# A decode block on one core: w3 in one DMA behind wo's row 12, the moved wq columns in two DMAs, x for the residual in two parts on the sync queue

## The chip, the core and the metric

The kernel runs on one core of a Trainium2 chip. The metric is device microseconds of one execution, median of several runs. The profile is one such execution; its span (136.1 us before) leaves out a little of what the time holds.

## The reference

Four tokens pass through one pre-norm block: layer norm, attention over the last 2048 positions of a cache, a residual, layer norm, a gated MLP, a residual. Everything is bf16 at the interface.

```
x: (4, 1, 1024)   wq: (1024, 4096)   k, v cache: (4, 4, 8192, 128), last 2048 used
wo: (4096, 1024)  w1, w3: (1024, 3584)  w2: (3584, 1024)

h  = x + softmax(q k^T * 128**-0.5) v @ wo      with q = layernorm(x) @ wq, 32 heads on 4 kv heads
h2 = h + (silu(layernorm(h) @ w1) * (layernorm(h) @ w3)) @ w2
```

With four tokens every weight is used once, so 55.6 MB have to be read for very little arithmetic.

## The kernel before

All weights and the cache pass through one ring of 160 KiB in each partition. A list says what is loaded where, in order; a call of `load_next` puts the next loads on the sync queue. The framework adds the waits: a load into bytes that are still to be read waits for their last reader. The last 512 columns of the last wq row of each partition are loaded apart from the rest, in 128 pieces of 1 KB on few DMA engines; these are the "moved columns" (`side` in the code).

```python
CE = 512
SETS = [(0, 5, 4), (80, 3, 2), (104, 3, 2)]

def load_side(r0, ne, ns):      # the last 512 columns of each partition's last wq row, as rows of their own
    t = ktpool.tile([P, JG * QD * 16], BF16, tag="kT")
    rows = A_wq[r0 * KC : (r0 + ne * 4 * ns) * KC, N_Q - CE : N_Q]
    rows = rows.rearrange("(t i k) n -> k i t n", i=ne, k=KC)[KC - 1]
    nc.sync.dma_start(out=t[: ne * 4, : ns * CE], in_=rows)
    ...
plan = [
    ("wq", load_rows, (0, wq_v, N_Q, 0, 4)),
    ("side", load_side, SETS[0]), ("side", load_side, SETS[1]), ("side", load_side, SETS[2]),
    ("wq", load_tail, (32 * KIB, wq_v, N_Q, 4, 4)),          # without those 512 columns
    ("k", ...), ("k", ...), ("v", ...),                      # two loads each
    ("v", load_kv, (0, A_v_cache, 2)),
    ("wo", load_rows, (32 * KIB, wo_v, D, 0, 32)),
    ("w1", load_rows, (96 * KIB, w1_v, N_F, 0, 8)),
    ("w3", load_rows, (0, w3_v, N_F, 0, 4)),
    ("w3", load_rows, (28 * KIB, w3_v, N_F, 4, 4)),
    ("w2", load_rows, (56 * KIB, w2_v, D, 0, 17)),
    ... # three more parts of w2
]
x_sb = act.tile([B, D], BF16)
nc.scalar.dma_start(out=x_sb[:], in_=x_flat)                 # x for the layer norm
load_next(8)
...
x_q = act.tile([P, CG], BF16)                                # x for the residual
nc.vector.memset(x_q[:], 0.0)
nc.scalar.dma_start(out=x_q[0:P:RS, :], in_=x_flat.rearrange("b (j c) -> j b c", j=JG))
...
# attention output, over b and j:   OT_ps += v[b][:, j, :] x P
        if b % BS == BS - 1:
            load_next()                                      # w1, then w3's first half
...
# y_ps += o4[i] x wo[i], i = 0..31
        if i == 11:
            load_next()                                      # w3's second half
load_next()                                                  # w2, first 17 rows
...
gate_up("w1", g_ps)                                          # after row 3: load_next(3), the rest of w2
...                                                          # silu on ACT and DVE
gate_up("w3", u_ps)
nc.vector.tensor_tensor(out=hg[:], in0=u_ps[:, :, :HF], in1=gs[:], op=ALU.mult)
nc.vector.transpose(out=hgT..., in_=hg...)                   # then y2 += hgT[i] x w2[i], i = 0..27
```

## Time and profile before

| | before |
|---|---|
| time, median of 3 (range) | 137.84 us (137.83 to 138.2) |
| bytes read from HBM | 55.59 MB, mean 409 GB/s over the span |
| complete landing of: first wq rows / wq tail | 12.84 / 23.57 us |
| wo / w1 | 82.02 / 98.91 us |
| w3, first and second half | 107.36 / 115.82 us |
| first part of w2 / last part of w2 | 126.08 / 132.79 us |

The landings are read from the semaphore increments in the trace: each DMA engine that carries part of a transfer adds one when its part is in, so a transfer over all engines shows 16 times, of which the last one counts. The page's lines and the stretches that carry the argument stand in the prediction below, with what to see in each. Two more lines of the kernel before will be needed, the start of the statistics and the first q matmuls in the timeline (columns: start, length, engine, line, operation, in brackets the idle time ahead and what ended it):

```profile
2.81 0.68 DVE L177 BATCH_NORM_STATS2 stats<-x_sb 4x6 f32<-4x512 bf16 x1 [0.33 <-DMA x_sb<-in_A_x_dram]
...
12.88 0.60 PE L260 MATMUL q_ps<-ring,xnT 128*4 128x512 bf16 x4 [6.49 <-DMA ring<-in_A_wq_dram]
```

The PE had idled for 6.49 us when wq came, so x was there long before.

### The profile page before, as it was taken

How to read it: one execution, taken by the hardware profiler on the slowest of the kernel's cores; microseconds unless marked ns; L12 is line 12 of the kernel's file. 1: busy time of each engine (PE TensorE's matmuls, PEld its weight loads, DVE VectorE, ACT ScalarE, POOL GpSimd, SP SyncE). 2: the span in 40 equal slices, each digit the busy share in tenths (PEclk: the TensorE clock that was granted, in tenths of full speed). 3: DMA queues.
4: the chain of work that ended last, by engine and by line, in shares of the span. 5: the costliest groups of instructions: out<-in, count | busy, mean ns of one | idle time of the engine just before them, and what ended most of it. 6: DMA issues, size and time to landing. Idle time of an engine off the chain costs nothing.

```text
span 136.1 us, 2438 instructions
## 1 busy us (share of the span) xinstructions
PE 72.9 (54%) x1096; PEld 45.1 (33%) x1096; DVE 44.1 (32%) x81; ACT 31.0 (23%) x36; POOL 1.7 (1%) x8
## 2 busy tenths in 40 slices
PE   0202980979898989800545906791096440900881
PEld 0200220267474737400034905470042220300760
DVE  5830000044252434471983001206100695080010
ACT  3000000016555555518376200000003300000000
POOL 5000000000000000000000000000000000000000
PEclk9999999999999999996555555589658686555589
DMA  5999999999999999999979999989899999989970
GB/s 157 463 464 413 414 401 419 443 419 438 419 434 434 424 443 419 429 527 458 482 328 443 482 409 405 477 388 460 354 421 426 455 438 451 430 389 403 434 292 5
DMA packets 2789, 55.75 MB, mean 410 GB/s; under 512 B 311, under 2 KB 471, under 8 KB 731
## 3 DMA queue, kind: packets, MB, share of 16 engines
q1 hardware_dynamic: 2731, 55.58, 95.5%
q8 instruction: 8, 0.13, 0.3%
q10 hardware_dynamic: 48, 0.02, 0.1%
q14 instruction: 2, 0.02, 0.0%
HBM read 55.59 MB, written 0.01 MB: 409 GB/s over the span
## 4 chain that ended last, share of the span: by engine, by line
DMA 55%; PE 23%; ACT 11%; DVE 5%; SPq 2%; issue 1%; ACTq 0%
DMA ring<-in_B_w_dram 40%; DMA ring<-in_A_wq_dram 15%; PE kt_ps L316 10%; ACT kT L322 5%; PE scores_ps L301 5%; ACT z L357 3%; PE q_ps L260 3%; SPq L120 2%; PE g_ps L456 2%; DVE rmax L333 2%; ACT Pm L338 2%; PE OT_ps L379 2%; DVE pT L347 1%; DVE z L353 1%; ACT L338 1%
## 5 line engine op out<-in xcount | busy, mean ns | idle before, releaser
L322 ACT COPY kT<-kt_ps 128x1024 bf16<-128x1024 bf16 x16 | 15.9, 1013 | 13.0 <-PE kt_ps L316 13.0
L316 PE MATMUL kt_ps<-ident,ring 128*128 128x128 bf16 x256 | 17.6, 228 | 0.0
L316 PEld LDWEIGHTS <-ring 128*128 128x128 bf16 x256 | 15.7, 103 | 4.9 <-issue 4.9
L320 DVE COPY kT<-kt_ps 128x1024 bf16<-128x1024 bf16 x16 | 11.1, 692 | 16.0 <-PE kt_ps L316 16.0
L260 PE MATMUL q_ps<-ring,xnT 128*4 128x512 bf16 x63 | 7.2, 627 | 10.1 <-DMA ring<-in_A_wq_dram 10.1
L379 PE MATMUL OT_ps<-z,ring 128*128 128x32 bf16 x256 | 7.5, 188 | 9.3 <-ACT z L357 5.0
L456 PEld LDWEIGHTS <-hnT 128*32 128x32 bf16 x128 | 5.3, 137 | 19.4 <-issue 16.7
L301 PE MATMUL scores_ps<-kT,qz 128*32 128x512 bf16 x64 | 9.9, 609 | 2.9 <-ACT kT L322 2.9
L456 PE MATMUL u_ps<-ring,hnT 128*32 128x448 bf16 x64 | 6.2, 567 | 8.6 <-DMA ring<-in_B_w_dram 8.6
L379 PEld LDWEIGHTS <-ring 128*128 128x128 bf16 x256 | 7.4, 105 | 10.0 <-issue 9.9
L456 PE MATMUL g_ps<-ring,hnT 128*32 128x448 bf16 x64 | 5.3, 515 | 5.4 <-DMA ring<-in_B_w_dram 5.4
L489 PEld LDWEIGHTS <-hgT 128*32 128x32 bf16 x156 | 4.5, 120 | 9.6 <-issue 8.8
L489 PE MATMUL y_ps<-ring,hgT 128*32 128x256 bf16 x68 | 3.8, 418 | 7.2 <-DMA ring<-in_B_w_dram 7.2
L278 DVE TENSOR_SCALAR q_sb<-q_ps 128x512 bf16<-128x512 f32 x1 | 0.7, 692 | 19.2 <-PE q_ps L260 19.2
L260 PEld LDWEIGHTS <-xnT 128*4 128x4 bf16 x63 | 2.0, 116 | 14.4 <-issue 14.3
L511 ACT CAST res<-yb_ps 128x128 bf16<-128x128 f32 x1 | 0.3, 266 | 26.6 <-PE yb_ps L489 26.6
L357 ACT ACTIVATE z<-pt_ps,mask 128x512 bf16<-128x512 f32 x8 | 5.3, 687 | 3.5 <-DVE z L353 3.5
L349 PE MATMUL pt_ps<-pT,perm 128*128 128x512 bf16 x4 | 2.4, 608 | 6.8 <-DVE pT L347 6.8
L279 ACT ACTIVATE q_sb<-q_ps 128x512 bf16<-128x512 f32 x1 | 0.6, 597 | 23.3 <-DVE q_sb L278 23.3
L353 DVE TENSOR_SCALAR z<-pt_ps,mask 128x512 bf16<-128x512 f32 x8 | 5.5, 741 | 1.2 <-ACT z L357 0.8
L470 DVE RECIPROCAL eg<-eg 128x896 f32<-128x896 f32 x1 | 5.8, 5753 | 0.0
L408 PE MATMUL y_ps<-ring,o 128*32 128x256 bf16 x128 | 5.3, 345 | 0.8 <-DVE o L395 0.8
(85 smaller groups left out, 54.7 us busy)
## 6 DMA issues: line engine op xcount, KB each, us to landing
ring<-in_A_k_cache_dram SPq DMA_DIRECT2D x4, 2048.0 KB, 25.3
ring<-in_A_v_cache_dram SPq DMA_DIRECT2D x4, 2048.0 KB, 39.1
ring<-in_B_w_dram SPq DMA_DIRECT2D x1, 7168.0 KB
ring<-in_B_w_dram SPq DMA_DIRECT2D x2, 3584.0 KB, 23.3
ring<-in_B_w_dram SPq DMA_DIRECT2D x1, 4352.0 KB
ring<-in_A_wq_dram SPq DMA_DIRECT2D x1, 4096.0 KB, 12.1
ring<-in_A_wq_dram SPq DMA_DIRECT2D x1, 3968.0 KB, 19.8
ring<-in_B_w_dram SPq DMA_DIRECT2D x1, 1792.0 KB
```

What stands on the lines that cost most here:

```text
L260: nc.tensor.matmul(q_ps[QD * g : QD * g + B, hf * 512 : hf * 512 + n], lhsT=xnT[:, kc, :], rhs=wq_t[:, c0 : c0 + n], start=(kc == 0), stop ...
L301: nc.tensor.matmul(scores_ps[QD * g : QD * (g + 1), n * 512 : (n + 1) * 512], lhsT=qz_v[:, z0 : z0 + QD], rhs=kT_v[:, g, :, :], start=(b = ...
L316: nc.tensor.transpose(out=kt_ps[:, jj, :], in_=k_v[:, n * NJ + t * TB + jj, :], identity=ident[:])
L320: nc.vector.tensor_copy(out=kT[:, t * TB : (t + 1) * TB, :], in_=kt_ps[:])
L322: nc.scalar.copy(out=kT[:, t * TB : (t + 1) * TB, :], in_=kt_ps[:])
L353: nc.vector.tensor_scalar(out=z[:, :, g, :], in0=pt_ps[:], scalar1=mask[:, g : g + 1], scalar2=None, op0=ALU.mult)
L357: nc.scalar.mul(out=z[:, :, g, :], in_=pt_ps[:], mul=mask[:, g : g + 1])
L379: nc.tensor.matmul(OT_ps[:, b, :], lhsT=loaded["v"][b][:, j, :], rhs=PTz[j // NJ][:, (j % NJ) * B + b, :, :], start=(j == 0), stop=(j == J ...
L408: nc.tensor.matmul(y_ps[QD * j : QD * (j + 1), :], lhsT=o4[:, i, :, :].rearrange("p b s -> p (b s)"), rhs=loaded["wo"][i][:, j * CG : (j + ...
L456: nc.tensor.matmul(out_ps[QD * j : QD * (j + 1), hf, :HF], lhsT=hnT[:, k, :], rhs=loaded[kind][k][:, c0 : c0 + HF], start=(k == 0), stop=( ...
L470: nc.vector.reciprocal(out=eg[:], in_=eg[:])
L489: nc.tensor.matmul(out_ps[QD * j : QD * (j + 1), :n], lhsT=hgT[:, i, :], rhs=loaded["w2"][i][:, j * CG + c0 : j * CG + c0 + n], **kw,)
```

## The change

It has three parts that share one idea: fewer and differently placed DMA issues for the same bytes. w3 becomes one transfer, which may only start when wo's first 12 rows, whose place it takes, are used up. Two of the three moved-column loads are joined. x for the layer norm comes in two halves on the scalar queue, and x for the residual moves to the sync queue, in two parts.

```diff
-    SETS = [(0, 5, 4), (80, 3, 2), (104, 3, 2)]
+    SETS = [(0, 5, 4), (80, 3, 4)]
...
-        ("side", load_side, SETS[2]),
...
-        ("w3", load_rows, (0, w3_v, N_F, 0, 4)),
-        ("w3", load_rows, (28 * KIB, w3_v, N_F, 4, 4)),
+        ("w3", load_rows, (0, w3_v, N_F, 0, 8)),
...
-    nc.scalar.dma_start(out=x_sb[:], in_=x_flat)
-    load_next(8)
+    for c in range(2):
+        nc.scalar.dma_start(out=x_sb[:, c * 512 : (c + 1) * 512], in_=x_flat[:, c * 512 : (c + 1) * 512])
+    load_next(7)
...
-    nc.scalar.dma_start(out=x_q[0:P:RS, :], in_=x_flat.rearrange("b (j c) -> j b c", j=JG))
+    for c in range(2):
+        nc.sync.dma_start(
+            out=x_q[c * 2 * QD : (c + 1) * 2 * QD : RS, :],
+            in_=x_flat.rearrange("b (j c) -> j b c", j=JG)[2 * c : 2 * c + 2],
+        )
...
-        if b % BS == BS - 1:
+        if b == 1:
             load_next()
```

## The prediction

> **What bounds the kernel now.** I read the page's slices first, to see which resource is full over the whole span; then stretches between landings, to see whether it is full everywhere; then the sync queue's issues and waits, to see how early each transfer is queued; last the timeline around the places that the change touches.
>
> ```profile
> PE 72.9 (54%) x1096; PEld 45.1 (33%) x1096; DVE 44.1 (32%) x81; ACT 31.0 (23%) x36; POOL 1.7 (1%) x8
> ...
> DMA  5999999999999999999979999989899999989970
> ```
>
> No engine is busy for much over half of the span, while the DMA row is at 9 from the second slice to the last but two. The stretches (columns: from:to, length, busy time of PE, PEld, DVE, ACT, POOL with counts, granted clock, DMA share, GB/s) say at what rate:
>
> ```profile
> 23.60:62.70 39.10, 30.72 (x359) 19.51 (x358) 14.50 (x20) 18.49 (x19) 0.00 (x0) 1.00 1.02 436
> 62.70:82.00 19.30, 8.28 (x192) 6.17 (x192) 8.27 (x14) 8.15 (x12) 0.00 (x0) 0.50 1.01 438
> ...
> 98.90:115.90 17.00, 8.38 (x100) 4.02 (x103) 7.47 (x3) 2.20 (x2) 0.00 (x0) 0.70 1.01 435
> 115.90:131.00 15.10, 7.59 (x140) 4.89 (x143) 3.22 (x3) 0.00 (x0) 0.00 (x0) 0.51 0.97 417
> 131.00:132.80 1.80, 1.58 (x60) 1.23 (x49) 0.00 (x0) 0.00 (x0) 0.00 (x0) 1.00 0.48 187
> ```
>
> The stream runs at about 435 GB/s and the last stretch falls to 187. The landing events in the trace (one semaphore increment for each DMA engine that took part) sharpen this: wo is complete at 82.02 us and w1 at 98.91, so w1's 7.34 MB took 16.89 us, or 435 GB/s; w3's halves land at 107.36 and 115.82 (8.46 us for 3.67 MB, 434 GB/s). So every transfer starts where the last one ends, and **the end is the sum of the bytes over a saturated stream**. It is the slowest DMA engine that counts: the first wq load's 16 increments lie 0.47 us apart, all later loads' about 1.8 us, to the last one (131.00 to 132.79). What lies between is the moved wq columns: 128 pieces of 1 KB, 46 ns each in the trace, on few engines. Their landings show 5 increments for the first set and 3 for each of the others, so the engines in all three carry 16 + 8 + 8 = 32 pieces, 32 x 46 ns = 1.5 us more than the others. That lag stays to the end and explains the 187 GB/s.
>
> The chain of waits seems to say otherwise for the middle (K transposes, softmax), but it follows w1 back to its issue at 75.79 us, and w1 could not have moved before wo was in at 82.02: the compute chain has some 6 us to spare. The sync queue's issues and waits:
>
> ```profile
> 75.79 0.33 SPq L94 DMA_DIRECT2D ring<-in_B_w_dram  x1
> ...
> SPq L94 <- PE OT_ps L379: 7.8, 1, 7.8
> ...
> 89.03 0.33 SPq L94 DMA_DIRECT2D ring<-in_B_w_dram  x1
> ...
> SPq L94 <- PE y_ps L408: 4.6, 1, 4.6
> ...
> 91.27 0.33 SPq L94 DMA_DIRECT2D ring<-in_B_w_dram  x1
> ```
>
> w1 goes out at 75.79, w3's second half at 89.03 (it waited for wo's row 12), the first part of w2 at 91.27; the queue does not need w3 until w1 is in at 98.91.
>
> **What the Trainium skill says.** All on the page "DMA: Bandwidth & Descriptors". Its Specifications give a fabric ceiling of 435 GB/s and an HBM limit near 358 for a core; the trace sits on the first (435 for w1), the second is not seen here. "Queues, rings and completion order" says that a DMA engine takes turns between queues packet by packet. The trace agrees: the residual's x, issued on the scalar queue at 1.35 us, has all 20 of its packets only between 6 and 11.3 us, one turn per wq packet (about 1.2 us each):
>
> ```profile
> q10 hardware_dynamic: 20, 0.01, 0.6%
> ```
>
> "Why a DMA increments its semaphore by 16 and not by 1" says that the number of engines is the largest count up to 16 that divides the slowest dimension of both sides; the 5 and 3 increments above fit sets with 5 and 3 row groups. "Issuing engines are not separate DMA queues" says that another queue saves only issue time; so moving x cannot add bandwidth, and no run yet shows it here.
>
> **The change part by part.**
>
> 1. *w3 in one DMA behind wo's row 12.* Bytes equal. It is issued where the second half was, about 89.0 us, and must be queued before 98.91: 9.9 us spare, no gap. It lands where the second half did, about 115.8. What it costs is early work:
>
> ```profile
> 107.40 3.01 PE L456 MATMUL u_ps<-ring,hnT 128*32 128x448 bf16 x32 [3.13 <-DMA ring<-in_B_w_dram]
> ...
> 115.86 3.18 PE L456 MATMUL u_ps<-ring,hnT 128*32 128x448 bf16 x32 [5.44 <-DMA ring<-in_B_w_dram]
> ...
> 119.08 1.09 DVE L475 TENSOR_TENSOR hg<-u_ps,gs 128x896 bf16<-128x896 f32 x1 [4.86 <-PE u_ps L456]
> 120.21 1.70 DVE L478 STREAM_TRANSPOSE hgT<-hg 128x896 bf16<-128x896 bf16 x1
> 126.18 3.55 PEld L489 LDWEIGHTS <-hgT 128*32 128x32 bf16 x69 [7.95 <-issue]
> 126.21 3.82 PE L489 MATMUL y_ps<-ring,hgT 128*32 128x256 bf16 x68 [7.17 <-DMA ring<-in_B_w_dram]
> ```
>
> The first 32 matmuls now wait with the others: 115.86 + 3.01 + 3.18 = 122.05, product 1.09 and transpose 1.70 with two gaps of 0.04, so hgT is ready near 124.9 instead of 121.91. The down projection waits for w2's first part until 126.08 anyway: **3.0 us later, 1.2 us still spare**, cost 0.
>
> 2. *The moved columns in two DMAs.* The second set has 3 row groups still, so by the rule it stays on 3 engines with 16 pieces each: 16 + 16 = 32 as before. One issue of 0.72 us on the sync queue goes, beside the first wq transfer: gain 0. Two small DVE copies go (one of xs, one of xsT), ahead of use: gain 0.
>
> 3. *x for the statistics in two halves on the scalar queue.* The first is issued at 0.73 as before; the second at about 1.35, where the residual's x was, and should meet the same turns: data near 6.1, increment near 7.4, landed near 7.7 instead of 2.8 us. From there the second statistics, the normalisation and the transposes to xnT took 6.31 - 2.81 = 3.5 us, less 0.66 for the first half: xnT near 10.6. The first wq load lands at 12.84: **some 4.3 us later, about 2.2 us still spare**, cost 0.
>
> 4. *The residual's x on the sync queue.* The compiled order has both parts after the second v load, and each DMA reuses the completion semaphore of the one eight before it. So the second part waits for the wq tail (23.57), and the last two v loads for the first two k loads (28.43 and 33.42), up to 13 us later than now. They are not needed in the stream before the second v load is in at 52.73: 19 us spare, cost 0. Each part has 8 rows from 2 groups, so 2 engines with 4 pieces of 512 B each; both parts make 8 pieces on engines that are already among the late ones, against 4 on the scalar queue before: 4 x 27 ns = +0.11 us. Increments cost 9 ns each: two more for these, two fewer for the dropped side and w3 loads, 0.
>
> Sum: 0 + 0 + 0 + 0.1 = **+0.1 us, 137.9 us**.
>
> **The rivals.** (a) *The down projection becomes bound by the PE.* hgT would have to slip by more than 1.2 us beyond the estimate. For it: the granted clock is 0.50 there, and 1.2 us is little. Against: both matmul times used are measured, the second one at 0.50, so nothing slower is in sight. It would add perhaps 0.5 us, since the last parts of w2 leave the PE slack as well. (b) *x arrives too late.* It would take over two more turns of 1.2 us; even then the q matmuls have slack before the wq tail at 23.57, so 0. (c) *The queue runs dry* because w3 waits for wo's row or v waits for k: 9.9 and 19 us speak against; a gap would cost its full length. (d) *A gain*, from fewer transfers or a scalar queue that gets out of the way of the wq load: at 435 GB/s with equal bytes I see at most tenths, -0.3 us or so.
>
> **Range and chances.** The three runs of before span 137.83 to 138.2, so 0.4 us is noise; with (a) upwards and (d) downwards, 137.5 to 138.5. Two per cent is 2.8 us, which no step comes near: within 2% has 0.97, slower 0.02 for an unseen gap in the stream, faster 0.01.
>
> **What would show it.** One u_ps group of 64 matmuls from about 115.8 us, hgT ready near 125 and y_ps still released by the DMA near 126.2; the second x_sb statistics near 7.7 us and q_ps still released by wq near 12.9; 432 to 438 GB/s between landings; v issues at about 28 and 33 us. The prediction is wrong if y_ps is released by hgT, if the DMA row shows a new gap, or if the lag of the last landing (1.8 us) has changed by over 0.3 us.

## The result, and the profile after

The changed kernel takes 137.94 us (median of 6 runs, 137.79 to 137.97), the kernel before 137.88 us in 6 runs. The ratio is 0.9999 with a 95% interval of 0.9986 to 1.0012. Ratios here are the mean time of one kernel's fast runs over that of the other's fast runs of the same rounds, so they are not quite the ratio of the medians. The change costs and gains nothing that can be measured: less than 0.2 us either way.

The page's engine line and DMA row of the changed kernel:

```profile
PE 72.3 (53%) x1096; PEld 46.1 (34%) x1096; DVE 43.9 (32%) x79; ACT 31.0 (23%) x36; POOL 1.7 (1%) x8
...
DMA  5999999999999999999989999989989899999970
```

The DMA row is as full as before. The stretches say the same (columns as in the prediction):

```profile
23.60:62.70 39.10, 31.16 (x359) 19.89 (x358) 14.49 (x20) 18.01 (x19) 0.00 (x0) 0.85 1.02 436
62.70:82.00 19.30, 8.28 (x192) 6.16 (x192) 8.27 (x14) 8.63 (x12) 0.00 (x0) 0.50 1.02 441
...
131.00:132.80 1.80, 1.80 (x70) 1.57 (x64) 0.00 (x0) 0.00 (x0) 0.00 (x0) 0.85 0.46 179
```

435 GB/s or a little over in the middle, and the thin last stretch, 179 GB/s, is there again. What has moved is work inside the slack. The second half of the gate (the product with w3, and its transpose to hgT, which the down projection y_ps needs) in the timeline:

```profile
115.70 5.95 PE L459 MATMUL u_ps<-ring,hnT 128*32 128x448 bf16 x64 [11.03 <-DMA ring<-in_B_w_dram]
121.71 1.09 DVE L478 TENSOR_TENSOR hg<-u_ps,gs 128x896 bf16<-128x896 f32 x1 [7.09 <-PE u_ps L459]
122.83 1.70 DVE L481 STREAM_TRANSPOSE hgT<-hg 128x896 bf16<-128x896 bf16 x1
126.06 3.82 PE L492 MATMUL y_ps<-ring,hgT 128*32 128x256 bf16 x68 [4.40 <-DMA ring<-in_B_w_dram]
```

All 64 matmuls now wait for w3 and run in one group, hgT is ready at 122.83 + 1.70 = 124.53 us (121.91 before), and y_ps is still released by the DMA, at 126.06 us. The head of the timeline, and what the scalar queue carried in the stretch from 6 to 11.3 us (packets, MB, share):

```profile
7.92 0.68 DVE L180 BATCH_NORM_STATS2 stats<-x_sb 4x6 f32<-4x512 bf16 x1 [4.90 <-DMA x_sb<-in_A_x_dram]
...
12.94 0.60 PE L263 MATMUL q_ps<-ring,xnT 128*4 128x512 bf16 x4 [2.03 <-DMA ring<-in_A_wq_dram]
```

```profile
q10 hardware_dynamic: 8, 0.00, 0.3%
```

Eight packets, 4 of data and 4 increments, are x's second half: it is used at 7.92 us instead of about 3.5 us, and the PE's idle time ahead of q shrinks from 6.49 to 2.03 us, but wq still ends it. The sync queue's issues:

```profile
33.41 0.56 SPq L102 DMA_DIRECT2D ring<-in_A_v_cache_dram  x1
...
76.27 0.33 SPq L94 DMA_DIRECT2D ring<-in_B_w_dram  x1
...
88.76 0.33 SPq L94 DMA_DIRECT2D ring<-in_B_w_dram  x1
```

The last v load goes out at 33.41 us (23.63 before), w1 at 76.27, w3 at 88.76, all ahead of need. The residual's x shows two increments for each of its parts (two engines each), the last ones at 52.67 and 52.86 us; it is used after 91 us.

### The profile page after: what moved, and what is told of

Its sections match the earlier page's. It is cut to its first block, busy times and chain, and to the rows that moved or that the text cites. A ratio compares the mean times of both kernels' runs of the same rounds, so it can differ in the third digit from the quotient of the medians.

```text
span 136.0 us, 2436 instructions
## 1 busy us (share of the span) xinstructions
PE 72.3 (53%) x1096; PEld 46.1 (34%) x1096; DVE 43.9 (32%) x79; ACT 31.0 (23%) x36; POOL 1.7 (1%) x8
## 4 chain that ended last, share of the span: by engine, by line
DMA 54%; PE 25%; ACT 11%; DVE 5%; SPq 2%; issue 1%; ACTq 0%
DMA ring<-in_B_w_dram 38%; DMA ring<-in_A_wq_dram 15%; PE kt_ps L319 11%; ACT kT L325 5%; PE scores_ps L304 5%; ACT z L360 3%; PE q_ps L263 3%; DVE rmax L336 2%; ACT Pm L341 2%; PE OT_ps L382 2%; DVE pT L350 1%; SPq L120 1%; PE g_ps L459 1%; DVE z L356 1%; ACT L341 1%
## 5 line engine op out<-in xcount | busy, mean ns | idle before, releaser
L263 PE MATMUL q_ps<-ring,xnT 128*4 128x512 bf16 x63 | 6.7, 595 | 7.8 <-DMA ring<-in_A_wq_dram 7.8
L459 PE MATMUL g_ps<-ring,hnT 128*32 128x448 bf16 x64 | 5.9, 558 | 4.9 <-DMA ring<-in_B_w_dram 4.9
L411 PE MATMUL y_ps<-ring,o 128*32 128x256 bf16 x128 | 5.9, 371 | 0.8 <-DVE o L398 0.8
L194 PE MATMUL tp_ps<-ident,xn 4*128 4x4 bf16 x8 | 0.7, 200 | 10.0 <-DVE xn L187 10.0
L411 PEld LDWEIGHTS <-o 128*32 128x32 bf16 x128 | 4.4, 131 | 3.1 <-DVE o L398 1.9
```

Source lines behind the costliest of these rows:

```text
L263: nc.tensor.matmul(q_ps[QD * g : QD * g + B, hf * 512 : hf * 512 + n], lhsT=xnT[:, kc, :], rhs=wq_t[:, c0 : c0 + n], start=(kc == 0), stop ...
L411: nc.tensor.matmul(y_ps[QD * j : QD * (j + 1), :], lhsT=o4[:, i, :, :].rearrange("p b s -> p (b s)"), rhs=loaded["wo"][i][:, j * CG : (j + ...
L459: nc.tensor.matmul(out_ps[QD * j : QD * (j + 1), hf, :HF], lhsT=hnT[:, k, :], rhs=loaded[kind][k][:, c0 : c0 + HF], start=(k == 0), stop=( ...
```

## The experiments

Twelve kernels ran. The theory was the prediction's: a saturated stream of fixed bytes, ended by its slowest DMA engine, with slack under everything that the change moves. Each run attacks one statement of it. The ratios are to the kernel before, which ran in the same rounds; the changed kernel, which differs from it by less than 0.2 us, was not run again.

### Are the moved columns the lag at the end?

```diff
-        ("side", load_side, SETS[0]),
-        ("side", load_side, SETS[1]),
-        ("wq", load_tail, (32 * KIB, wq_v, N_Q, 4, 4)),
+        ("wq", load_rows, (32 * KIB, wq_v, N_Q, 4, 4)),
```

(and the matmuls and transposes of the moved columns go, the wq matmuls take all columns).

> The changed kernel without moved wq columns: the last four wq rows come whole, in one DMA over all engines, and the two column loads and their 8 matmuls go. Theory of the prediction (the 32 pieces of 1 KB on a few engines are the lag that the last landing shows): every engine carries 8 KB more (0.3 us) but the late engines lose 1.5 us, so the last landing comes about 1.2 us earlier, near 131.5 us, and the time is near 136.7 us. Rival (other engines are made late too, by the program's instruction fetches of 16 KB on the same engines, and they end the stream just as late): the end moves by 0 to +0.3 us, time 137.9 to 138.2, and the spread of the last landing stays near 1.7 us.

It took 138.09 us (5 runs), ratio 1.0014 (1.0001 to 1.0026), so about 0.2 us **slower** (just clear of the noise), which is what the rival said. The last stretch is thinner still:

```profile
131.00:132.90 1.90, 1.63 (x64) 1.28 (x52) 0.00 (x0) 0.00 (x0) 0.00 (x0) 1.00 0.37 146
```

The landing increments show why (all in us; the spread of the 16 increments of one transfer):

```
                              changed kernel                        without moved columns
wq tail        21.76 to 23.62, five engines late      22.01 to 22.41, none late
second k load  31.49 to 33.35                         fifteen 31.72 to 32.11, one 33.69
third v load   55.81 to 57.74                         thirteen 56.08 to 56.49, three 57.89 to 57.92
last w2 part   four 130.94 to 131.56,                 eight 131.07 to 131.50, one 132.14,
               twelve 132.24 to 132.68                seven 132.73 to 132.90
```

So the moved columns do make five engines late at the wq tail, as predicted, and without them none is. But then single engines drop behind by some 1.5 us, one after another. In the stretch from 28 to 33 us of this run the profile has this queue besides the big one:

```profile
q8 instruction: 1, 0.02, 1.2%
```

One packet of 16 KB, at 31.24 us: the program's own instructions being fetched. The single packets in the trace show what it does. On one engine a packet of k ends at 31.24 us, the fetch runs from 31.24 to 32.20, and the next packet of k, from 32.19 to 33.26, takes 1.08 us where all others take 0.61: 0.96 + 0.47 = 1.4 us, and this engine's increment comes last, at 33.69.

Seven such fetches come before 110 us (31.2, 43.3, 54.8, 77.7, 84.4, 90.8 and 107.6 us) and one of 8 KB at 59.6 us; at the end seven engines are late and one is half late. The count fits the changed kernel too. Three engines carry 32 of the moved pieces and two carry 16. With seven fetches of 16 KB before 110 us, and one of 8 KB at 60.63 us that by the landings falls on an engine with 16 pieces, 3 + 7 + 1 = 11 engines should be late, and eleven are in the last but one part of w2 (131.63 to 132.06 us). An eighth fetch, at 130.63 us, fits the twelfth in the last part.

The Trainium skill, page "Runtime: NRT & Kernel Launch", section "Instruction fetch mechanics", says that instructions are refilled in blocks of 16 KiB over the sequencer's own DMA queue and that this is mostly hidden. The trace agrees on the size; but the DMA engine that serves a fetch carries its share of the weights later. That fetches cause all the steps is read from the one engine followed above and from the counts, not from a run with other fetches.

With the rival right, the moved columns are useful: every engine loses 8 KB (0.3 us at its share of 435 GB/s) and a few engines, which by the count above the large fetches do not hit, take them over and end no later than the ones that are hit. Why the fetches miss these engines stays open.

### Does one slow engine set the end?

```diff
+            dummy = A_k_cache[0, 0, 0:512, :].rearrange("(a b) d -> a (b d)", b=4)
+            nc.sync.dma_start(
+                out=ring[:, 152 * KIB : 153 * KIB],
+                in_=dummy.rearrange("(t i) n -> i t n", i=2),
+            )
```

behind w1; the control has `in_=dummy`. A first form wrote to a tile of its own behind the residual's x:

> The changed kernel with one more load of 128 KB behind the residual's x, into a tile that nobody reads, in 128 pieces of 1 KB laid out so that two engines carry 64 each. Theory (each DMA engine has its own rate and the slowest one sets the end): 64 x 46 ns = 2.9 us more on two late engines, so +2.9 us, 140.8 us. Rival (the engines share one ceiling of 435 GB/s, so only the bytes count): 131 KB / 435 GB/s = +0.3 us, 138.2 us.

> The control for the last one: the same 128 KB in the same 128 pieces, 8 on each of 16 engines. Theory: 8 x 46 ns = +0.37 us, 138.3 us. Rival (shared ceiling): +0.3 us as well. A time near that of two engines would say that the extra DMA as such costs, not where its pieces lie.

They took 142.52 us (median of three fast runs, ratio 1.0384; a fourth run was slow) and 141.91 us (1.028), both far over either theory, and both runs are **confounded**. The extra tile made the scheduler change the PE's order. In the timeline with two engines, K transposes run ahead of the moved columns' matmuls:

```profile
28.34 4.45 PE L321 MATMUL kt_ps<-ident,ring 128*128 128x128 bf16 x48 [11.91 <-DMA ring<-in_A_k_cache_dram]
...
33.31 2.18 PE L275 MATMUL q_ps<-t,xsT 20*4 20x512 bf16 x8 [0.25 <-DVE xsT L220]
```

Those matmuls use up what v's place holds, so a v load waited 16.6 us for the PE, and w1 went out at 81.17 us (81.33 in the control, where wo's load waited). The second form leaves PE, DVE and ACT as they are.

> A cleaner form of the load on two engines: the same 128 pieces of 1 KB, 64 on each of two engines, now from contiguous memory into free bytes behind w1, queued between w1 and w3; the order on PE, DVE and ACT is that of the changed kernel. Theory (each engine has its own rate, the slowest sets the end): 64 x 46 ns = +2.9 us, 140.8 us, with two increments of the last landing some 3 us behind the others. Rival (one shared ceiling): +0.3 us, 138.2 us.

> Its control: the same pieces, 8 on each of 16 engines, in the same place. Theory and rival both: 131 KB at 435 GB/s to 8 x 46 ns, +0.3 to +0.4 us, 138.2 to 138.3 us.

On two engines: ratio 1.0254 (1.0238 to 1.027), +3.5 us. Spread over 16: 138.27 us, ratio 1.0028 (1.0014 to 1.0041), +0.4 us. The same bytes in the same pieces cost nine times as much on two engines as on sixteen, so a ceiling on the bytes alone is refuted, and the cost is near what the theory says if **the slowest engine sets the end**. The size is 0.6 us over the 2.9 us expected. The profiled run with two engines fell in the slow state (its w3 packets took 2.38 us in place of 2.12 on all engines), so no size is read from its trace. Its order agrees: two increments come last in the landing of w3 (120.50 and 120.64 us, the one before at 119.50). What the 0.6 us are stays open, and so does whether the pieces slow the other engines as well: no fast trace of this kernel exists.

### Does w3's later issue cost anything, and what would a gap cost?

```diff
-        if i == 11:
-            load_next()
-    load_next()
...
-                load_next(3)
+                load_next(5)
```

> The changed kernel with w3 (and the first part of w2 after it) issued behind w1's row 3, at about 100.5 us, after w1 has landed at 98.8 us, in place of 88.8 us. Theory (an issue costs nothing until the stream runs dry, and then the whole gap): the data of w1 end about 0.4 us before the landing, the first packet comes about 1.0 us after the issue, so a gap of some 3.1 us, +3 us, 141.0 us. Rival (some of the gap is hidden by slack of the compute, as with the other waits): +1.5 us or less.

This was a **miss of the experiment**: 137.72 us, ratio 0.9987 (0.9973 to 1.0). The compiled order of the engines that compute is that of the changed kernel, and w3 did not go out at 100.5 us:

```profile
86.41 0.33 SPq L94 DMA_DIRECT2D ring<-in_B_w_dram  x1
```

A load's place in the program text sets only its turn on the queue. What it waits for is the last reader of its bytes, wo's row 12. The run serves as a near repeat of the changed kernel (w3 goes out 2.4 us earlier) and shows the noise: 0.13%. For a true delay, GpSimd has to write into the place after w1 has landed:

```diff
         if i == 11:
+            nc.gpsimd.tensor_copy(out=ring[:, 0:1], in_=loaded["w1"][0][:, 0:1])
             load_next()
+    nc.gpsimd.tensor_copy(out=ring[:, 56 * KIB : 56 * KIB + 1], in_=loaded["w1"][0][:, 0:1])
     load_next()
```

> The changed kernel with w3 and w2's first part made to wait for w1's landing: GpSimd copies one element of w1 into the first byte of each of their places before they are overwritten (the loads then overwrite it). Theory (an issue is free until the stream runs dry, then the gap counts in full): w1 lands at 98.8 us, its data end 0.4 us before, copy and issue 0.3 us, first packet 1.0 us after: w3's data start near 100.2 in place of 98.4 us on the late engines, +1.8 us, 139.7 us. Rival (slack elsewhere hides it): +0.5 us or less.

It took 142.27 us, ratio 1.0317 (1.0303 to 1.0331): +4.4 us, more than twice the theory's 1.8.

```profile
99.24 0.19 POOL L419 COPY ring<-ring 128x1 bf16<-128x1 bf16 x1 [96.94 <-DMA ring<-in_B_w_dram]
99.36 0.19 POOL L421 COPY ring<-ring 128x1 bf16<-128x1 bf16 x1
99.45 0.81 SPq L94 DMA_DIRECT2D ring<-in_B_w_dram  x2
```

The issue comes at 99.45 us, and w3's first packets start on all 16 engines between 100.40 and 101.14 us. Six engines had ended w1 between 96.55 and 97.31 us, the other ten between 97.93 and 98.67, so the late ones lost 2 us or a little more (that is the theory's part), the early ones 3 to 4. The first packets after the gap are slow as well: they take 2.1 to 3.5 us where a packet of w3 takes 2.12 in the running stream, and end between 103.23 and 104.03 us, where the late engines of the changed kernel had ended theirs near 100.4. **The wait for the whole of w1 lines all engines up again**, and the early ones' lead is gone. Fifteen engines land w3 between 118.38 and 119.11 us, some 3 us behind the late engines of the changed kernel, and the one left over at 120.25 us; an instruction fetch at 105.74 us lies between. In the changed kernel the fetch at 105.23 us does not show in the last landing of w3 (115.66 us): six engines are early at w1 and five at w3, so it took one early engine's lead. So of the 4.4 us some 3 are the gap with its slow restart, on all engines, and the rest is a fetch that no lead hides; this split is read from the landings, not tested.

### How much slack did the gate have, and how much did the change use?

The transpose to hgT is repeated two or four times, in the changed kernel and in the one before.

```diff
+    nc.vector.transpose(   # two or four times, the same output
+        out=hgT[:].rearrange("p i x -> p (i x)"),
+        in_=hg[:].rearrange("q s c -> q (s c)").rearrange("q (c i) -> q i c", i=IF),
+    )
```

> The changed kernel with the transpose to hgT done three times (two more of 1.70 us each, on the path). hgT is ready at 124.5 us in the changed kernel, w2's first part at 125.9. Theory (the change has used up 2.6 us of the 4.2 us that the gate had to spare): hgT at 128.0, y_ps starts 2.0 us later, of which the later parts of w2 hide 0.3 us, +1.5 to 1.8 us, 139.5 us; y_ps is then released by hgT and not by the DMA. Rival (still hidden): 137.9 us. The kernel before with the same two transposes should keep its time (a later run).

137.95 us, ratio 1.0009 (0.9991 to 1.0027). The expected +1.5 us did not come, although y_ps is now released by hgT:

```profile
127.42 3.41 PE L500 MATMUL y_ps<-ring,hgT 128*32 128x256 bf16 x68 [6.40 <-DVE hgT L489]
```

It starts 1.36 us later than in the changed kernel but takes 3.41 us instead of 3.82, and the rest of w2's matmuls follow without waiting, so the PE catches up with the last loads. A released wait is not yet a longer time. Some of this is luck of the clock: the granted clock in this trace is 0.58 over the y_ps group and 1.00 from 130.83 us on (0.50 and 0.85 in the changed kernel), and it is the fastest of four runs from 137.78 to 138.46 us, so a cost of up to 0.4 us is not excluded. With four:

> The changed kernel with four more transposes to hgT on the path in place of two. With two, y_ps was released by hgT at 127.42 us and the matmuls then ran at the full clock and just caught up with the last loads. Theory (no slack is left there): 2 x 1.73 us = +3.5 us, less at most 0.2 us, so 141.2 us. Rival (the stream still hides some): under 140 us.

> The kernel before with the same four more transposes. Theory (w3 in two DMAs gave hgT 2 to 2.6 us earlier, which is what the change uses up): hgT at 121.9 + 6.9 = 128.8 us, 1.4 us later than the 127.4 us that was still hidden, so 139.0 to 139.3 us, about 2 us under the changed kernel with four. Rival (the two halves of w3 have no use): the same as the changed kernel with four.

The changed kernel took 141.99 us, ratio 1.0287 (1.0251 to 1.0323), +4.0 us; the kernel before 139.94 us, ratio 1.0145 (1.0115 to 1.0174), +2.0 us. The y_ps groups of the two:

```profile
130.75 3.82 PE L508 MATMUL y_ps<-ring,hgT 128*32 128x256 bf16 x68 [9.86 <-DVE hgT L497]
```

```profile
129.05 3.82 PE L505 MATMUL y_ps<-ring,hgT 128*32 128x256 bf16 x68 [9.86 <-DVE hgT L494]
```

Both are 0.6 to 0.8 us over their theory. It had counted on the full clock for the matmuls behind the wait, which was not granted: 0.50 over both groups, and after them 0.50 and then 0.77 in the changed kernel, 0.92 in the kernel before. So the two halves of w3 are worth some 2 us of slack to the kernel before (1.7 us in the start of y_ps; the clock, and the other parts of the change, may have a share in the rest), and nothing of time as long as the slack is not needed. (With two more transposes the kernel before was not run: with four it is already closer to its time than the changed one.)

### Is x late for q, and does w3 alone hide something?

```diff
-    for c in range(2):
-        nc.scalar.dma_start(out=x_sb[:, c * 512 : (c + 1) * 512], in_=...)
+    nc.scalar.dma_start(out=x_sb[:, :512], in_=x_flat[:, :512])
     load_next(7)
...
+    nc.scalar.dma_start(out=x_q[0:P:RS, :], in_=x_flat.rearrange("b (j c) -> j b c", j=JG))
+    nc.scalar.dma_start(out=x_sb[:, 512:], in_=x_flat[:, 512:])
```

> The changed kernel with the residual's x back on the scalar queue as one DMA, between the halves of x for the statistics, so that the second half meets five more turns of 1.24 us. Theory (there is slack behind xnT too): second statistics near 14 us in place of 7.9, xnT near 17 us in place of 10.8, q_ps released by xnT at 17 us in place of wq at 12.9, but q ends at 27.8 in place of 27.2 us and the stream stays full: 137.9 us. Rival (x on the path): + 4 us.

137.81 us, ratio 0.9996 (0.9981 to 1.0012).

```profile
13.21 0.68 DVE L176 BATCH_NORM_STATS2 stats<-x_sb 4x6 f32<-4x512 bf16 x1 [10.17 <-DMA x_sb<-in_A_x_dram]
...
16.17 3.58 PE L259 MATMUL q_ps<-ring,xnT 128*4 128x512 bf16 x32
...
23.71 3.56 PE L259 MATMUL q_ps<-ring,xnT 128*4 128x512 bf16 x31 [1.86 <-DMA ring<-in_A_wq_dram]
```

x really is the last to come here, 3.3 us after wq, and the second group of q matmuls still waits for wq's tail: even a late x costs nothing.

The last run takes the kernel before with w3 in one DMA and nothing else:

```diff
-        ("w3", load_rows, (0, w3_v, N_F, 0, 4)),
-        ("w3", load_rows, (28 * KIB, w3_v, N_F, 4, 4)),
+        ("w3", load_rows, (0, w3_v, N_F, 0, 8)),
...
-        if b % BS == BS - 1:
+        if b == 1:
```

> The kernel before with w3 in one DMA behind wo's row 12 and nothing else of the change. Theory: cost 0, 137.9 us, y_ps still released by the DMA. Rival (a gain or loss of w3 that the other parts cancel): 0.2 us or more from the kernel before, either way.

137.86 us (5 runs), ratio 1.0004 (0.9992 to 1.0017). No gain or loss of w3's is being cancelled by the other parts. The x part and the two column loads were not run alone.

## Why the prediction was right, and where its working was not

The predicted time, 137.9 us, and the claim that every step is hidden hold.

- **w3 in one DMA.** Right in each number: issue 88.76 (89.0 predicted), hgT at 124.53 us (124.9), y_ps released by the DMA. The spare time was undersized: "1.2 us still spare" measured 126.06 - 124.53 = 1.5 us ahead of the DMA, and up to another 1.4 us beyond it, since 1.36 us of delay in y_ps cost less than 0.4 us. Rival (a) would have needed nearly 3 us, not 1.2. The other spare time was oversized: "9.9 us spare" for the issue counts to w1's last increment, but the first engine had its share of w1 in at 96.66 us, 7.9 us after the issue at 88.76.
- **Moved columns in two DMAs.** Right: the joined set still shows 3 increments. Cost 0 was not tested alone.
- **x in halves.** Right: 7.92 us (7.7) for the second statistics, xnT at 10.84 (10.6), q released by wq at 12.94 with 2.0 us to spare (2.2). More slack lies behind it, as the run with x after wq shows.
- **The residual's x on the sync queue.** The issue times are right (v at 28.56 and 33.41 us). Its term, "4 x 27 ns = +0.11 us", can't be told from 0: the interval of the result is some 0.2 us wide to either side, and the last landing even came 0.1 us earlier in the changed kernel's trace (132.68 against 132.79 us).
- **The DMA row** was read as 9 "from the second slice to the last but two"; four of these slices are at 7 or 8. The rates of the stretches carry the argument without it.
- **The step that failed** is in the part on what bounds the kernel: "That lag stays to the end and explains the 187 GB/s", said of the moved columns. Their lag is real at the wq tail, but taking it away made the kernel 0.2 us slower. At the end twelve engines are late, not the few with moved columns, and without moved columns seven or eight still are. The prediction overlooked instruction fetches: seven of 16 KB before 110 us, which make seven engines late. This did not hurt the total, because the change leaves the lag alone; a proposal built on it (drop the moved columns for 1.2 us) would have lost.
- **Rival (c)** was undersized too: "a gap would cost its full length". A gap of 2 us on the late engines cost 4.4 us: by the landings, the restart was slow and a later fetch met engines without a lead.

## What to carry to other kernels

On a stream that is full from end to end, the place and number of issues cost nothing here, where every load was queued before the first engine had ended the one ahead of it; read that margin from the issue times, and do not judge it by the share of busy time or by the chain of waits. Read the completion of a transfer engine by engine: the last increment sets the end, and a lag seen early need not be the lag at the end, so take it away once before building on it. And an experiment that delays a load needs a real dependency; moving its line in the program moved nothing here, while an unrelated extra tile reordered another engine.

## What the Trainium skill lacked or had wrong

- "Runtime: NRT & Kernel Launch" ("Instruction fetch mechanics") calls the cost of a 16 KiB boundary "mostly hidden"; it lacks that the fetch takes its turn on a DMA engine that is loading weights, and what that costs there: 0.96 us for the fetch at 31.24 us and 0.47 us more for the packet behind it. In the run without moved columns, seven 16 KB fetches went with seven engines that ended about 1.5 us late (132.73 to 132.90 against 131.07 to 131.50 us).
- "DMA: Bandwidth & Descriptors" ("Queues, rings and completion order") has the turns but not their length in a loaded stream: beside wq packets of 32 KB each turn of the scalar queue took 1.24 us, and the first one came at 6.12 us for an issue made before 1.6 us.
- The same page ("Where 436 GB/s comes from") says that for HBM to SBUF the HBM side, about 358 GB/s, binds, without the condition that the page gives just above (both cores of an HBM domain streaming). One core alone ran at 435 GB/s here, which is the page's fabric figure; its own single-core measurement of 425 GB/s fits better.
- The same page ("Rules for kernel authors") lacks that a wait for a whole transfer levels the engines, and that the first packets after a gap are slow (2.1 to 3.5 us against 2.12): a gap of 2 us on the late ones cost 4.4 us.
